# Thirty-two early rows of a weight matrix: from partitions four apart in two regions to partitions eight apart in one

## The chip, the cores and the metric

One core of a Trainium2 chip runs the kernel. The metric is device microseconds of one execution, as a median over executions; lower is better. TensorE (PE) multiplies matrices into PSUM, VectorE (DVE) and ScalarE (ACT) compute, GpSimd (POOL) fills constants, and SyncE (SP) issues nearly all transfers from device memory (HBM) to on-chip memory (SBUF, 128 partitions). The core has 16 DMA engines.

## The reference

One decode step for 8 sequences, in float32. The layer-normed input feeds attention over a given cache and a dense layer with the Mish activation; both are added to the input.

```python
x = A_x                                   # (8, 1, 512)
xn = layernorm(x)
q = (xn @ wq)                             # 32 heads of 128
k, v = k_cache, v_cache                   # (8, 8 kv heads, 8192, 128), 4 query heads on each
p = softmax(q @ k^T * 128**-0.5)
a = (p @ v) @ wo                          # wo: (4096, 512)
h = xn @ w1 + b1                          # 512 -> 1792
b = (h * tanh(softplus(h))) @ w2          # 1792 -> 512
return x + a + b
```

The two caches are 2 x 268 MB; everything else that is read is about 24 MB.

## The kernel before

The work is cut into 32 units `j` (4 pairs of key/value heads by 8 sequences, `b = j % 8`). Each unit has a load of keys and a load of values, 8.4 MB each, as tiles of 128 partitions by 16384 floats (`load_unit`); they share the tile `kv`, in which each load waits until the tensor before it has been consumed. In one turn of the loop PE does the scores of unit `j` (L339), the softmax's small steps, the values of unit `j - 1` (L411), and a turning of the weights `e` (L378); SP issues the value load of `j`, then extra transfers if there are any, and in the next turn the key load of `j + 2`. SP issues its transfers in program order, and one that waits for a buffer holds those behind it.

After the loop come `wo` in four tiles (L634), `w2` in five pieces (L640), and the output. The sum of the four `wo` products, two per head pair and row block, is built up in the PSUM tile `H` (`few`, `outputs`, `down_long`), then folded to `O`, to which the last pieces of `w2` are added (L567) before VectorE adds the input (L664) and SP stores it.

**The early rows.** Each tile of `wo` is 128 partitions of four pieces of 1024 floats. Of head pair 0 the fourth piece of all rows, and of pair 1 the last 384 floats of it (`FEWC`), are not loaded after the loop with the rest but during it: `FEW1` and `FEW2` list small transfers, `load_few` issues them behind the value load of the unit given in the list. They go into `ws`, the tile of `wq`, which is free by then. There are 32 rows `q` of each pair, and a row of the transfer is four runs of 4 KB (pair 0) or of 1.5 KB (pair 1). A transfer has `k` = 5 or 3 rows; in the program's reckoning its first row is one share of work, its second row another, and so on.

Before, a transfer's rows stand four partitions apart, from partition `t` (0 to 3) for the five-row ones. The three-row ones stand from partition 32 + `t` for pair 0; for pair 1 they stand at `t` too, in a second slot further along the partition. `turn_few(m)` brings the attention output of the pair into the matching order with two matmuls against columns of the identity (20 and 12 rows), each followed by a VectorE copy to `oF`. `few(m)` multiplies: eight products over 44 rows for pair 0, at the end of unit 27; eight over 20 rows for pair 1, after the loop.

Counting a row of pair 0 as 1 and one of pair 1 as 384/1024 = 0.375, the five places of a transfer carry 11, 11, 11, 5.5 and 5.5 of 44.

Of the kernel before, what the change touches and what calls it, by code (L numbers as in the profile page):

```python
# [8 lines left out]
F32 = mybir.dt.float32  # L9
# [4 lines left out]
P = 128  # L14
B = 8
D = 512
# [8 lines left out]
G = 4  # L25
NH = 2
TG = SK // (NH * G) // P
BW = 1024
CC = D // P
FG = F // G  # L30
FT = 4
FP = FG // FT
Q = P // G
# [33 lines left out]

FEW1 = [(t, 5, t, 22 + t // 2, 0) for t in range(4)]  # L70
FEW1 += [(32 + t, 3, 20 + t, 24 + t // 2, 0) for t in range(4)]
FEW2 = [(t, 5, t, 28 + t // 2, 0) for t in range(4)]
FEW2 += [(t, 3, 20 + t, 30, 1) for t in range(4)]
EARLY = 27
FEWC = 384

# [5 lines left out]
def kernel(  # L82
# [12 lines left out]
    nc = tc.nc  # L95
    PSUM = bass.MemoryType.PSUM

    const = ctx.enter_context(tc.tile_pool(name="const", bufs=1))
# [5 lines left out]
    ws = const.tile([P, CC * BW], F32, name="ws")  # L104
# [4 lines left out]
    M = psum.tile([P, 512], F32, name="m")  # L109
    H = psum.tile([P, 512], F32, name="h")  # L110

    ident = const.tile([P, P], F32, name="ident")
# [12 lines left out]
    oT = const.tile([P, H2, B], F32, name="oT")  # L125
# [1 line left out]

    x8 = oX.rearrange("p m i h b -> p (m i h b)")[:, : W1R * 2 * B]
    x8 = x8.rearrange("p (i h b) -> p i h b", i=W1R, h=2)
    oF = const.tile([48, 2, CC, 2, B], F32, name="oF")  # L130
    aT = const.tile([P, 2 * W2R, B], F32, name="aT")
    pt8 = const.tile([P, HALF, PL * TL, H2], F32, name="pt8")
    tr = const.tile([P, PL * TL, 32], F32, name="tr")
# [1 line left out]
    def load_q(m):  # L135

        rows = wq.rearrange("j p f -> (j p f)").rearrange("(m p f) -> m p f", m=NP, p=P)
        nc.sync.dma_start(ws, rows[m])

    def load_unit(src, j, at):  # L140
        m, b = divmod(j, B)
        lo = (b * HKV + 2 * m) * NH * G
        t = kv[:, at : at + ROW]
        nc.sync.dma_start(
            t,
            src[lo : lo + NB].rearrange("j p f -> (j p f)").rearrange("(p f) -> p f", p=P),
        )
        return t
# [7 lines left out]
    rows = wq.rearrange("j p f -> (j p f)").rearrange("(m p f) -> m p f", m=NP, p=P)[0]  # L156
# [2 lines left out]
    nc.scalar.dma_start(ws[:, half:], rows[:, half:])  # L159
    b1_sb = kv[:G, W1_AT + 7168 : W1_AT + 7168 + FG]  # L160

    for lo in range(0, FG, 150):
        hi = min(lo + 150, FG)
        nc.scalar.dma_start(b1_sb[:, lo:hi], b1.rearrange("(g f) -> g f", g=G)[:, lo:hi])
    k_t = {0: load_unit(kT, 0, V_AT)}
    w1_t = kv[:, W1_AT : W1_AT + 7168].rearrange("p (i f) -> p i f", i=W1R)
# [3 lines left out]
    nc.gpsimd.memset(ones, 1.0)  # L170
    nc.gpsimd.memset(perm, 0.0)
    nc.gpsimd.memset(pt8, 0.0)
    nc.gpsimd.memset(oF, 0.0)
    for t in (H, M):
        nc.vector.memset(t, 0.0)
    nc.vector.reduce_sum(bsel, ident.rearrange("p (g q) -> p q g", g=G), axis=AX.X)
# [1 line left out]
    def more_constants():  # L178
        nc.vector.reduce_sum(mask, ident.rearrange("p (x d) -> p x d", x=NB), axis=AX.X)
        nc.vector.reduce_sum(  # L180
            hmask, ident.rearrange("p (c h q) -> p h c q", c=CC, h=2), axis=AX.XY
        )
        nc.vector.memset(O, 0.0)
        for g in range(4):

            src = ident.rearrange("p (c d u g h) -> p d u g c h", c=2, d=2, u=2, g=4)
            dst = perm[:, g].rearrange("p (d u g c h) -> p d u g c h", d=2, u=2, g=4, c=2)
            for d in range(2):
                nc.vector.tensor_copy(dst[:, d, :, g], src[:, d, :, g])
        nc.vector.reduce_sum(hsel, ident.rearrange("p (c h) -> p h c", h=H2), axis=AX.X)  # L190
        nc.vector.reduce_sum(
            isel, ident.rearrange("p (c t h) -> p t c h", t=TL, h=H2), axis=AX.XY
        )
        for d in range(2):
            nc.vector.reduce_sum(
                rsel[:, d * REP : (d + 1) * REP],
                ident.rearrange("p (c d k h) -> p d h c k", c=2, d=2, h=REP)[:, d],
                axis=AX.XY,
            )
        nc.vector.tensor_copy(  # L200
            gsel, ident[:G, :G].rearrange("p (g o) -> p g o", o=1).to_broadcast([G, G, B])
        )
# [128 lines left out]
    def scores(j, k, first, part):  # L331

        w = WK[j]
        lo = 0 if first else DI // 2
        kk = k.rearrange("p (i c f) -> p i c f", i=DI, c=HALF)
        for n in range(DI // 2):
            i = lo + n
            for c in range(HALF):
                nc.tensor.matmul(  # L339
                    S[64 * c : 64 * (c + 1), :],  # L340
                    w[:, i].rearrange("p d k h -> p (d k h)"),
                    kk[:, i, c, :],
                    start=(part == 0 and n == 0),
                    stop=(part == 1 and n == DI // 2 - 1),
                )
# [80 lines left out]
    def merge(j, os):  # L426
        m, b = divmod(j, B)
        nc.tensor.matmul(M[:, 168 : 168 + H2], os, hsel, start=True, stop=True)  # L428
        nc.vector.tensor_mul(oT[:, :, b], M[:, 168 : 168 + H2], RT.pop(j))
# [61 lines left out]
        nc.vector.tensor_copy(aT, turned.rearrange("p (j q) -> p j q", q=Q)[:, :, :B])  # L491


    def load_few(m, p, k, q, slot):

        rows = wo[4 * m : 4 * (m + 1)].rearrange("u p f -> (u p f)")
        rows = rows.rearrange("(u q i f) -> q u i f", u=4, i=4, f=BW)
        n = FEWC if m else BW
        t = ws[p : p + 4 * k - 3 : 4, 4 * n * slot : 4 * n * (slot + 1)].rearrange(
            "p (u f) -> p u f", u=4  # L500
        )
        nu = 2 if m and k == 5 else 4
        for u in range(0, 4, nu):
            nc.sync.dma_start(
                t[:, u : u + nu], rows[q : q + 4 * k - 3 : 4, u : u + nu, 3, BW - n :]
            )

    def turn_few(m):

        o = oT.rearrange("p h b -> p (h b)")  # L510
        n = H2 * B
        parts = ((0, 20, 0, 0), (0, 12, 20, 1) if m else (32, 12, 20, 0))
        for p, r, lo, slot in parts:
            t = M[p : p + r, 384 + n * slot : 384 + n * (slot + 1)]
            nc.tensor.matmul(t, ident[:, 4 * lo + 3 : 4 * (lo + r) : 4], o, start=True, stop=True)
            if m:
                nc.vector.tensor_copy(
                    oF[p : p + r, 1].rearrange("p u h b -> p (u h b)").rearrange(
                        "p (s u b) -> p s u b", s=2, u=CC
                    )[:, slot],  # L520
                    t.rearrange("p (u h b) -> p u h b", u=CC, h=2)[:, :, 1],
                )
            else:
                nc.vector.tensor_copy(oF[p : p + r, 0].rearrange("p u h b -> p (u h b)"), t)

    def few(m):
        rows = (44, 20)[m]
        n = FEWC if m else D
        w = oF[:rows, m].rearrange("p u h b -> p (u h b)").rearrange("p (n b) -> p n b", b=B)
        for i in range(2 * CC):  # L530
            nc.tensor.matmul(
                H[Q * (i % G) : Q * (i % G) + B, D - n :],
                w[:, i],
                ws[:rows, i * n : (i + 1) * n],
                start=(m == 0 and i < G),
                stop=False,
            )

# [45 lines left out]
    for j in range(UNITS):  # L584
        b = j % B
        more = j // B + 1 < NP

        k = k_t.pop(j)
        low_first = j == 0 or j % 2 == 1
        scores(j, k, low_first, 0)  # L590
        if j == UNITS - 1:
            v_t[j] = load_unit(v, j, K_AT[0])
        elif j > 0:
            k_t[j + 1] = load_unit(kT, j + 1, K_AT[(j + 1) % 2])
        scores(j, k, not low_first, 1)
        WK.pop(j)
        softmax(j)
        os = None
        if j > 0:
            os = values(j - 1, v_t.pop(j - 1))  # L600
        if j > B and b == 1:
            turn_o(j // B - 1)
        if j == B + 1 or j == 2 * B + 1:
            turn_few(j // B - 1)
        if j + 1 < UNITS:
            v_t[j] = load_unit(v, j, V_AT)
            if more and b == SPREAD_Q:
                spread(qT)
            key_weights(j + 1)
        if j == 0:  # L610
            mish(w1_t, b1_sb, kv[:, W1_AT : W1_AT + 6 * FG])
        for m, rows in enumerate((FEW1, FEW2)):
            for p, k, q, at, slot in rows:
                if j == at:
                    load_few(m, p, k, q, slot)
        if more and b == LOAD_Q:
            load_q(j // B + 1)
        if more and b == MAKE_Q:
            qT = project(tr.rearrange("p y c -> p (y c)")[:, :512])
        turn(j)  # L620
        if j > 0:
            merge(j - 1, os)
        if more and b == SPREAD_Q - 1:
            selections()
        if j == EARLY:
            few(0)
# [3 lines left out]
    for m in range(NP):  # L630
        rows = wo[4 * m : 4 * (m + 1)].rearrange("u p f -> (u p f)")
        rows = rows.rearrange("(p f) -> p f", p=P)
        n = (3 * BW, 4 * BW - FEWC)[m] if m < 2 else 4 * BW
# [3 lines left out]
    parts = ((0, G), (G, 8), (8, 11), (11, 13), (13, 14))  # L637
    for lo, hi in parts:
        t = kv[:, W2_AT + lo * D : W2_AT + hi * D]
# [13 lines left out]
    for g in range(G):  # L653
# [4 lines left out]
            start=True,  # L658
            stop=False,
# [44 lines left out]
```

## Time and profile before

| | us |
|---|---|
| median of 3 runs | 1309.56 (1309.19 to 1310.08) |
| profiled execution, its own time | 1309.29 |
| its span, first to last instruction | 1307.5 |
| PE busy | 1087.8 (83%) |
| DVE busy | 346.4 (26%) |
| ACT busy | 44.4 (3%) |
| DMA, mean over the span | 430 GB/s |

Busy times are sums over an engine's instructions; a share of DMA is the mean over the 16 DMA engines. A view by windows gives, for a stretch of time, each compute engine's busy time with its instruction count, the clock granted to TensorE, the DMA engines' mean busy share and their rate. The chain of waits is followed back from the last instruction: each piece is either work or the transfer that was waited for.

### The profile page before, as it was taken

Reading aid. Unit: us, or ns where it says so; the run is one execution under the profiler, and the core shown is the slowest. Engines: PE = TensorE matmul, PEld = TensorE weight load, DVE = VectorE, ACT = ScalarE, POOL = GpSimd, SP = SyncE. Lnnn points to the kernel's source line nnn. Section 1 sums busy time; section 2 is a strip of 40 time slices with the busy share of each in tenths; the row PEclk is TensorE's granted clock in tenths of the full one; section 3 lists DMA queues with packets and bytes.
Section 4 is the critical chain, followed back from the end, with each engine's and each line's share of the span. In section 5 each row is a group of like instructions: output and inputs, shape, how many; then the busy total and the mean of one; then the engine's idle time right before and its main releaser. Section 6 shows DMA issues by size and latency. Waiting matters only on the chain.

```text
span 1307.5 us, 11114 instructions
## 1 busy us (share of the span) xinstructions
PE 1087.8 (83%) x5088; PEld 352.2 (27%) x5088; DVE 346.4 (26%) x547; ACT 44.4 (3%) x121; POOL 2.3 (0%) x10
## 2 busy tenths in 40 slices
PE   6988888878979789787887888787897797888786
PEld 4222222223323222222322222232232222222222
DVE  3341222321223221223131222212322311323212
ACT  1000000000000000000000000000000000000000
POOL 0000000000000000000000000000000000000000
PEclk9999888898989898888898888897988997988898
DMA  9999999999999999999999999999999999999998
GB/s 404 444 422 442 428 437 429 435 435 430 430 437 430 436 431 436 428 438 432 432 434 430 438 426 444 422 442 426 437 428 434 435 427 440 428 434 427 435 433 339
DMA packets 11946, 561.79 MB, mean 430 GB/s; under 512 B 1384, under 2 KB 1652, under 8 KB 2172
## 3 DMA queue, kind: packets, MB, share of 16 engines
q1 hardware_dynamic: 11732, 560.03, 99.2%
q10 hardware_dynamic: 168, 1.06, 0.2%
q8 instruction: 40, 0.66, 0.2%
q14 instruction: 6, 0.05, 0.0%
HBM read 561.01 MB, written 0.07 MB: 429 GB/s over the span
## 4 chain that ended last, share of the span: by engine, by line
DMA 72%; PE 26%; DVE 1%; issue 0%; ACT 0%; SPq 0%
DMA kv<-in_v 64%; PE o L411 18%; DMA kv<-in_kT 6%; PE s L339 6%; DMA kv<-in_w 2%; PE x L378 2%; PE h L457 1%; PE x L303 0%; DVE tr L394 0%; DVE nm L351 0%; DVE tr L396 0%; ACT qr L310 0%; PE o L567 0%; PE h L452 0%; DVE nr L355 0%
## 5 line engine op out<-in xcount | busy, mean ns | idle before, releaser
L339 PE MATMUL s<-kv,wk 128*64 128x512 f32 x2048 | 501.4, 652 | 90.0 <-DMA kv<-in_kT 51.0
L411 PE MATMUL o<-kv,pt 128*32 128x512 f32 x2048 | 267.0, 681 | 48.5 <-DMA kv<-in_v 45.7
L339 PEld LDWEIGHTS s<-kv,wk 128*64 128x64 f32 x2048 | 164.3, 151 | 404.4 <-issue 317.8
L378 PE MATMUL x<-e,perm 128*128 128x512 f32 x256 | 228.0, 1046 | 2.0 <-ACT qr L310 2.0
L351 DVE TENSOR_REDUCE nm<-s 128x1 f32<-128x512 f32 x32 | 22.1, 692 | 432.5 <-PE s L339 432.5
L411 PEld LDWEIGHTS o<-kv,pt 128*32 128x32 f32 x2048 | 69.7, 123 | 220.2 <-issue 168.2
L378 PEld LDWEIGHTS x<-e,perm 128*128 128x128 f32 x256 | 53.3, 219 | 143.1 <-issue 140.5
L394 DVE STREAM_TRANSPOSE tr<-x 128x2048 f32<-128x2048 f32 x32 | 73.1, 2285 | 54.4 <-PE x L378 54.4
L419 DVE TENSOR_SCALAR os<-o,isel 128x128 f32<-128x128 f32 x32 | 11.2, 351 | 275.3 <-PE o L411 275.3
L322 DVE TENSOR_TENSOR wk<-qr,mask 128x1024 f32<-128x1024 f32 (+1 forms) x33 | 62.8, 1902 | 18.7 <-ACT qr L310 18.7
L400 DVE TENSOR_TENSOR pt<-tr 64x512 f32<-64x512 f32 x64 | 43.9, 686 | 1.6
L367 ACT COPY nmx<-m 128x1 f32<-128x1 f32 x32 | 5.1, 159 | 1111.3 <-PE m L363 1111.3
L396 DVE TENSOR_TENSOR tr<-tr 128x1024 f32<-128x1024 f32 x32 | 39.2, 1225 | 1.1
L421 DVE SCALAR_TENSOR_TENSOR os<-o,isel,os 128x128 f32<-128x128 f32 x96 | 33.7, 351 | 3.4
L352 PE MATMUL m<-ident,nm 128*1 128x128 f32 x32 | 8.6, 270 | 25.3 <-DVE nm L351 25.3
L392 DVE RECIPROCAL rt<-m 128x16 f32<-128x16 f32 x16 | 4.1, 258 | 78.6 <-PE m L388 78.6
L363 PE MATMUL m<-ident,nx 1*128 1x1 f32 x32 | 7.0, 217 | 19.8 <-DVE nx L357 19.8
L370 ACT ACTIVATE e<-s,nmx 128x512 f32<-128x512 f32 x32 | 22.0, 687 | 1.0
L303 PE MATMUL x<-qT,tr 128*128 128x64 f32 x128 | 19.3, 315 | 3.0 <-ACT qr L310 2.7
L303 PEld LDWEIGHTS x<-qT,tr 128*128 128x128 f32 x128 | 18.1, 226 | 6.2 <-ACT qr L310 3.3
L428 PEld LDWEIGHTS m<-hsel,os 128*128 128x128 f32 x64 | 11.2, 196 | 27.6 <-issue 19.5
L373 DVE TENSOR_SCALAR lsel<-rsel,l 128x8 f32<-128x8 f32 x32 | 7.4, 231 | 42.0 <-ACT e L370 42.0
(107 smaller groups left out, 180.8 us busy)
## 6 DMA issues: line engine op xcount, KB each, us to landing
ws<-in_wq SPq DMA_DIRECT2D x3, 2048.0 KB
kv<-in_wo SPq DMA_DIRECT2D x2, 2048.0 KB
kv<-in_w SPq DMA_DIRECT2D x1, 3584.0 KB
kv<-in_w SPq DMA_DIRECT2D x2, 1024.0 KB
kv<-in_wo SPq DMA_DIRECT2D x1, 1856.0 KB
kv<-in_wo SPq DMA_DIRECT2D x1, 1536.0 KB
ws<-in_wq ACTq DMA_DIRECT2D x1, 1024.0 KB
ws<-in_wq SPq DMA_DIRECT2D x1, 1024.0 KB
```

Of the source, the lines that this page charges most:

```text
L303: nc.tensor.matmul(X[:, half, k * 64 : (k + 1) * 64], wide[:, half * 8 + k], qT, start=True, stop=True,)
L322: nc.vector.tensor_mul(w[:, i : i + n], q[:, i : i + n].to_broadcast([P, n, 2, NH * G, REP]), mask.rearrange("p (o d k r) -> p o d k r", o ...
L339: nc.tensor.matmul(S[64 * c : 64 * (c + 1), :], w[:, i].rearrange("p d k h -> p (d k h)"), kk[:, i, c, :], start=(part == 0 and n == 0), s ...
L351: nc.vector.tensor_reduce(nm, S, axis=AX.X, op=ALU.max, negate=True)
L370: nc.scalar.activation(e, S, AF.Exp, bias=nmx, accum_out=l)
L378: nc.tensor.matmul(X[:, g], perm[:, g], e.rearrange("p (t q l) -> p l t q", t=TL, q=PP), start=True, stop=True,)
L394: nc.vector.transpose(tr, X.rearrange("p g (y q) -> p y g q", q=PP))
L396: nc.vector.tensor_add(t[:, :, 0], t[:, :, 0], t[:, :, 1])
L400: nc.vector.tensor_add(pt8[half, :, :, d * REP : (d + 1) * REP].rearrange("p c y h -> p y c h"), t[:, 0], t[:, 1],)
L411: nc.tensor.matmul(O[Q * q : Q * (q + 1), :], pt8[:, c, TL * l : TL * (l + 1), :].rearrange("p t h -> p (t h)"), vt[:, 512 * n : 512 * (n ...
L421: nc.vector.scalar_tensor_tensor(os, O[:, DH * i : DH * (i + 1)], isel[:, i : i + 1], os, op0=ALU.mult, op1=ALU.add)
L457: nc.tensor.matmul(hp[Q * g : Q * g + B, :], x8[:, i, g // 2], w1_t[:, i, g % 2 * FG : (g % 2 + 1) * FG], start=False, stop=(i == W1R - 1),)
```

## The change

The rows stay the same 32 of each pair and so do their bytes; the places change. One list `FEW` holds for each pair its groups (first partition, width, rows per transfer, first row), and `FEW_AT` the unit behind which each transfer is issued. A transfer's rows now stand eight partitions apart. For pair 0 the five-row transfers start at partitions 0 to 3 and the three-row ones at 4 to 7, so that they interleave in one region of 36 partitions. For pair 1 there are six five-row transfers, starting at 0 to 5, and one of two rows, at 6 and 14, in a region of 38. The five places of a transfer now carry 10.625, 10.625, 10.25, 6.25 and 6.25.

`turn_few` uses one matmul against a selection matrix `fsel`, made at the start by four VectorE copies from the identity into a tile that GpSimd zeroes (it used to zero `oF`), and one copy. `few(1)` has four products over 38 rows in place of eight over 20. The small vector `b1` comes in two transfers on ACT's queue in place of three.

```diff
-FEW1 = [(t, 5, t, 22 + t // 2, 0) for t in range(4)]
-FEW1 += [(32 + t, 3, 20 + t, 24 + t // 2, 0) for t in range(4)]
-FEW2 = [(t, 5, t, 28 + t // 2, 0) for t in range(4)]
-FEW2 += [(t, 3, 20 + t, 30, 1) for t in range(4)]
+FEW = (((0, 4, 5, 0), (4, 4, 3, 20)), ((0, 6, 5, 0), (6, 1, 2, 30)))
+FEW_AT = ((22, 22, 23, 23, 24, 24, 25, 25), (28, 28, 29, 29, 30, 30, 30))
+FEWP = (36, 38)
...
-    for lo in range(0, FG, 150):
-        hi = min(lo + 150, FG)
+    for lo in range(0, FG, FG // 2):
+        hi = lo + FG // 2
...
-    nc.gpsimd.memset(oF, 0.0)
+    nc.gpsimd.memset(fsel, 0.0)
...
+        rows = ident.rearrange("p (q i) -> p i q", i=4)[:, 3]
+        for m in range(2):
+            for p, w, k, q in FEW[m]:
+                nc.vector.tensor_copy(
+                    fsel[:, m].rearrange("p (n t) -> p n t", t=8)[:, :k, p : p + w],
+                    rows[:, q : q + w * k].rearrange("p (n t) -> p n t", t=w),
+                )
...
-    def load_few(m, p, k, q, slot):
+    def load_few(m, p, k, q, w):
...
-        t = ws[p : p + 4 * k - 3 : 4, 4 * n * slot : 4 * n * (slot + 1)].rearrange(
-            "p (u f) -> p u f", u=4
-        )
+        t = ws[p : p + 8 * k - 7 : 8, : 4 * n].rearrange("p (u f) -> p u f", u=4)
+        last = q + w * (k - 1) + 1
...
-                t[:, u : u + nu], rows[q : q + 4 * k - 3 : 4, u : u + nu, 3, BW - n :]
+            nc.sync.dma_start(t[:, u : u + nu], rows[q:last:w, u : u + nu, 3, BW - n :])
...
     def turn_few(m):
-        parts = ((0, 20, 0, 0), (0, 12, 20, 1) if m else (32, 12, 20, 0))
-        for p, r, lo, slot in parts:
...
+        r = FEWP[m]
+        t = M[:r, 384 : 384 + n]
+        nc.tensor.matmul(
+            t, fsel[:, m, :r], oT.rearrange("p h b -> p (h b)"), start=True, stop=True
+        )
+        nc.vector.tensor_copy(oF[:r, m].rearrange("p u h b -> p (u h b)"), t)
...
     def few(m):
-        for i in range(2 * CC):
+        for i in range(m, 2 * CC, 1 + m):
+            q = i // (1 + m)
             nc.tensor.matmul(
-                H[Q * (i % G) : Q * (i % G) + B, D - n :],
-                w[:, i],
-                ws[:rows, i * n : (i + 1) * n],
+                H[Q * (q % G) : Q * (q % G) + B, D - n :],
+                oF[: FEWP[m], m, i // 2, i % 2],
+                ws[: FEWP[m], q * n : (q + 1) * n],
```

On SP, from the value load of unit 29 to the first tile of `wo`, the program before reads as follows (a row is a line, the tile written and the tensor read, the shape, and a count):

```order
L144 DMA kv<-in_v 128x16384
L504 DMA ws<-in_wo 5x2x384 x4
L144 DMA kv<-in_kT 128x16384
L144 DMA kv<-in_v 128x16384
L504 DMA ws<-in_wo 3x4x384 x4
L144 DMA kv<-in_v 128x16384
L634 DMA kv<-in_wo 128x3072
```

And now:

```order
L146 DMA kv<-in_v 128x16384
L513 DMA ws<-in_wo 5x2x384 x4
L146 DMA kv<-in_kT 128x16384
L146 DMA kv<-in_v 128x16384
L513 DMA ws<-in_wo 5x2x384 x4
L513 DMA ws<-in_wo 2x4x384
L146 DMA kv<-in_v 128x16384
L633 DMA kv<-in_wo 128x3072
```

Behind the value load of unit 30 stand five small transfers in place of four; all others keep their place and shape, and only the partitions they write differ, which such rows do not show.

On PE, from the last turning of the weights to the fold into `O`, before (`pt`: the turned weights, `os` and `oT`: the attention output):

```order
L378 MATMUL x_69<-e,perm 128x512 x4
L388 MATMUL m<-lsel,ones 128x16
L428 MATMUL m<-hsel,os 128x8
L531 MATMUL h<-ws,oF 8x384 x8
L411 MATMUL o<-kv,pt_90 32x512 x32
L544 MATMUL h<-kv,oX 8x512 x6
```

And now:

```order
L388 MATMUL x_69<-e,perm 128x512 x4
L398 MATMUL m<-lsel,ones 128x16
L438 MATMUL m<-hsel,os 128x8
L529 MATMUL h<-ws,oF 8x384 x4
L421 MATMUL o<-kv,pt_91 32x512 x32
L542 MATMUL h<-kv,oX 8x512 x6
```

Four products fewer stand ahead of the last unit's values; nothing else there has moved.

More of the change, by code (lines that the diff above doesn't have):

```diff
@@ L129 @@
     x8 = x8.rearrange("p (i h b) -> p i h b", i=W1R, h=2)
-    oF = const.tile([48, 2, CC, 2, B], F32, name="oF")
+    oF = const.tile([FEWP[1], 2, CC, 2, B], F32, name="oF")
+    fsel = const.tile([P, 2, 40], F32, name="fsel")
     aT = const.tile([P, 2 * W2R, B], F32, name="aT")
@@ L498, in load_few @@
         n = FEWC if m else BW
-        t = ws[p : p + 4 * k - 3 : 4, 4 * n * slot : 4 * n * (slot + 1)].rearrange(
-            "p (u f) -> p u f", u=4
-        )
+        t = ws[p : p + 8 * k - 7 : 8, : 4 * n].rearrange("p (u f) -> p u f", u=4)
+        last = q + w * (k - 1) + 1
         nu = 2 if m and k == 5 else 4
         for u in range(0, 4, nu):
-            nc.sync.dma_start(
-                t[:, u : u + nu], rows[q : q + 4 * k - 3 : 4, u : u + nu, 3, BW - n :]
-            )
+            nc.sync.dma_start(t[:, u : u + nu], rows[q:last:w, u : u + nu, 3, BW - n :])
     def turn_few(m):
-        o = oT.rearrange("p h b -> p (h b)")
         n = H2 * B
-        parts = ((0, 20, 0, 0), (0, 12, 20, 1) if m else (32, 12, 20, 0))
-        for p, r, lo, slot in parts:
[L514 to L524, printed above, removed]
+        r = FEWP[m]
[4 more added lines that the diff above has]
+        nc.vector.tensor_copy(oF[:r, m].rearrange("p u h b -> p (u h b)"), t)
     def few(m):
-        rows = (44, 20)[m]
         n = FEWC if m else D
-        w = oF[:rows, m].rearrange("p u h b -> p (u h b)").rearrange("p (n b) -> p n b", b=B)
-        for i in range(2 * CC):
+        for i in range(m, 2 * CC, 1 + m):
+            q = i // (1 + m)
             nc.tensor.matmul(
-                H[Q * (i % G) : Q * (i % G) + B, D - n :],
-                w[:, i],
-                ws[:rows, i * n : (i + 1) * n],
-                start=(m == 0 and i < G),
+                H[Q * (q % G) : Q * (q % G) + B, D - n :],
+                oF[: FEWP[m], m, i // 2, i % 2],
+                ws[: FEWP[m], q * n : (q + 1) * n],
+                start=(m == 0 and q < G),
                 stop=False,
@@ L611 @@
             mish(w1_t, b1_sb, kv[:, W1_AT : W1_AT + 6 * FG])
-        for m, rows in enumerate((FEW1, FEW2)):
-            for p, k, q, at, slot in rows:
+        for m in range(2):
+            rows = [(p + t, k, q + t, w) for p, w, k, q in FEW[m] for t in range(w)]
+            for row, at in zip(rows, FEW_AT[m]):
                 if j == at:
-                    load_few(m, p, k, q, slot)
+                    load_few(m, *row)
         if more and b == LOAD_Q:
```

## The prediction

> **What bounds the kernel now.** I read the page first, then the chain of waits, then the DMA engines' share by windows. The page:
>
> ```profile
> span 1307.5 us, 11114 instructions
> PE 1087.8 (83%) x5088; PEld 352.2 (27%) x5088; DVE 346.4 (26%) x547; ACT 44.4 (3%) x121; POOL 2.3 (0%) x10
> DMA packets 11946, 561.79 MB, mean 430 GB/s; under 512 B 1384, under 2 KB 1652, under 8 KB 2172
> q1 hardware_dynamic: 11732, 560.03, 99.2%
> q8 instruction: 40, 0.66, 0.2%
> DMA 72%; PE 26%; DVE 1%; issue 0%; ACT 0%; SPq 0%
> ```
>
> Queue q1, the one on which SP issues, fills 99.2% of the 16 DMA engines' time; 72% of the chain is transfers. PE is busy for 83%, but waits for loads in every unit. Only the DMA engines have no time left, so the end is set by whichever of the sixteen has most to do. The last pieces of the chain:
>
> ```profile
> 918.23 28.57 DMA kv<-in_v
> ...
> 1247.45 30.05 DMA kv<-in_v
> 1277.51 25.93 DMA kv<-in_w
> 1303.49 0.62 PE o L567 x16
> 1304.12 0.45 PE o L567 x8
> 1304.60 0.29 DVE os L664
> ```
>
> The last piece of `w2` lands at 1303.45 us and 1.4 us of work and the store follow. How the sixteen end is seen in windows (us of each engine, granted clock, DMA share, GB/s), with one window of the steady part ahead:
>
> ```profile
> 600.00:640.00 40.00, 34.37 (x153) 10.49 (x145) 11.92 (x16) 0.94 (x3) 0.00 (x0) 0.87 0.98 425
> 1297.20:1298.90 1.70, 1.21 (x12) 0.12 (x8) 0.00 (x0) 0.00 (x0) 0.00 (x0) 1.00 0.88 366
> 1300.40:1301.80 1.40, 1.06 (x32) 0.77 (x32) 0.00 (x0) 0.00 (x0) 0.00 (x0) 1.00 0.75 307
> 1302.00:1302.90 0.90, 0.66 (x24) 0.55 (x24) 0.00 (x0) 0.00 (x0) 0.00 (x0) 1.00 0.67 271
> 1303.00:1303.20 0.20, 0.09 (x4) 0.00 (x0) 0.00 (x0) 0.00 (x0) 0.00 (x0) 1.00 0.56 215
> 1303.20:1303.40 0.20, 0.00 (x0) 0.00 (x0) 0.00 (x0) 0.00 (x0) 0.00 (x0) 1.00 0.41 154
> 1303.40:1303.60 0.20, 0.11 (x4) 0.11 (x8) 0.00 (x0) 0.00 (x0) 0.00 (x0) 1.00 0.11 41
> 1303.60:1304.30 0.70, 0.69 (x24) 0.34 (x17) 0.00 (x0) 0.00 (x0) 0.00 (x0) 1.00 0.00 0
> ```
>
> In the steady part a busy engine moves 425 / (0.98 x 16) = 27.1 GB/s. At the end the share says how many still work: 14 of 16 after 1297.2, 12 after 1300.4, 11 after 1302.0, 9 after 1303.0, none after 1303.6. So two engines are 6 us ahead of the last, and about eleven end within 1.6 us of each other. The early rows use this lead: they put work on a few engines so that all have less at the end. In no row has an engine a name; I take it, as the program reckons, that row `i` of a small transfer is carried by engine `i`, so that 5 engines carry extra rows and 11 carry none.
>
> **The change, part by part.**
>
> *The shares.* A row of pair 0 is 4 x 4096 B, at 27.1 GB/s 0.60 us of an engine; one of pair 1, 4 x 1536 B, is 0.23 us. Engines 0 and 1 carry 0.375 x 0.60 = 0.23 us less, engine 2 carries 0.45 us less, engines 3 and 4 carry 0.45 us more; 11 engines carry the same. Of the nine that still work at 1303.0 at most three can be ones that lose work, so the others still end near 1303.5. I count 0; the bounds are a gain of 0.2 us (were the last ones engines 0 to 2) and a loss of 0.3 us (were engine 3 or 4 among them).
>
> *The partitions.* This is the part that can cost. A full load gives each engine eight of the 128 partitions. I take as working picture that these are four neighbours and the four that lie 32 higher, and call such a set an entry: engine `e` fills entry `e`, which for the first 32 partitions is p // 4. No row shows it. Then before, every early row lay in the entry of the engine that carried it (t + 4i and 32 + t + 4i). Now pair 0's five-row transfers lie in entries 0, 2, 4, 6, 0 and its three-row ones in 1, 3, 5; of pair 1 those from partitions 0 to 3 lie as the former, those from 4 and 5 in 1, 3, 5, 7, 1, and the last two rows in 1 and 3. In rows of pair 0, engine 1 carries 10.6 rows, all into entries that other engines fill, and its own entry takes 5.9 rows from others; for engine 2 it is 10.25 out and 5.5 in; for engine 4, 6.25 and 5.5; for 3, 6.25 and 5.1; for 0, 5.1 and 5.5.
>
> What sharing an entry costs, no row of this trace can show, since before nothing shares. If 27.1 GB/s is all that an entry takes in, then a row that meets the main stream takes twice its 0.60 us, and the entry's own engine loses 0.60 us as well. Ceiling, if every row meets a stream: engine 1 loses (10.6 + 5.9) x 0.60 = 10.0 us, engine 2 loses 9.5 us. Floor: a row meets none while the entry's engine is itself away with early rows. That can't be for engine 2's second-group rows (entry 5, whose engine carries no early rows: 4 + 2 x 0.375 = 4.75 rows) nor for engine 1's in entry 3 in the three-row and two-row transfers (4.4 rows), so at least 4.75 x 0.60 = 2.9 us. I take the middle, 6.4 us: the rows of one unit keep an engine about 1.2 us, and the windows show engines up to 6 us apart, so bursts that could miss each other will often not coincide. If instead 27.1 GB/s is the engine's own limit and the entry takes more, the cost is 0.
>
> The row says 27.1 GB/s for each busy engine and not where the limit sits. [...]
>
> *SP.* The early transfers keep their place behind the value loads; at unit 30 five stand in place of four.
>
> ```profile
> 1226.41 0.33 SPq L144 DMA_DIRECT2D kv<-in_v  x1
> 1226.79 3.05 SPq L504 DMA_DIRECT2D ws<-in_wo  x4
> 1247.45 0.34 SPq L144 DMA_DIRECT2D kv<-in_v  x1
> ```
>
> Four issues take 3.05 us here, so a fifth 0.8 us, and SP then stands until 1247.45: at least 16 us of cover (1229.84 to 1247.45), 0 on the path. Were the cover gone, the last value load would be issued 0.8 us later. The region for pair 1 lies where pair 0's was, as before, and waits for the same products of unit 27.
>
> *PE and VectorE.* `few(1)` loses half its products:
>
> ```profile
> 1274.78 1.66 PE L531 MATMUL h<-ws,oF 20*8 20x384 f32 x16
> 1279.31 8.77 PE L411 MATMUL o<-kv,pt 128*32 128x512 f32 x64 [2.88 <-DVE pt L400]
> ```
>
> It saves 0.8 us, and PE then waits 2.88 us for VectorE's L400 anyway: it will wait 3.7 us, and the path has nothing of it. The turning saves one matmul and one copy for each pair:
>
> ```profile
> L515 PE MATMUL m<-oT,ident 128*20 128x64 f32 x4 | 0.7, 270 | 4.0 <-DVE oX L444 4.0
> L515 PE MATMUL m<-oT,ident 128*12 128x64 f32 x4 | 0.7, 264 | 0.6 <-DVE oF L524 0.4 <-DVE oF L517 0.3
> ```
>
> That is 0.7 us of PE and 0.6 us of waiting over both pairs, behind the values and ahead of the next load's landing: 0, bounded by 1.3 us of gain if it stood on the path. Four new VectorE copies stand in the start, ahead of the query's copy:
>
> ```profile
> 2.74 0.20 POOL L173 MEMSET oF<- 48x128 f32 x1
> 12.07 0.62 DVE L189 COPY perm<-ident 128x16 f32<-128x16 f32 x8
> 17.55 0.22 DVE L296 TENSOR_SCALAR qT<-m 128x64 f32<-128x64 f32 x1 [3.95 <-PE m L288]
> 27.94 2.83 PE L339 MATMUL s<-kv,wk 128*64 128x512 f32 x6 [0.60 <-DMA kv<-in_kT]
> ```
>
> Eight like them took 0.62 us in a row, one by itself about 0.15, so four take 0.3 to 0.6 us. They need GpSimd's zeroes, which by the row of `oF` are there by 3 us, and lie ahead of 3.95 us in which VectorE waits for PE; the first scores wait for a load in the end. Cost 0; without that cover 0.6 us. One ACT-queue transfer less for `b1`: 0.
>
> *Sum.* The delayed engine starts from 0 to 0.5 us ahead of the last (the three windows from 1303.0), and gets up to 0.2 us from the new shares: I take 0.5 off. 1309.29 + 6.4 - 0.5 = 1315.2 us against the profiled execution's own time, which is 1.8 us over its span and 0.27 us under the median of the runs; on the median's scale **1315.5 us**. The bounds of this case are 2.9 - 0.5 and 10.0 - 0.5, so 1312.0 to 1319.1.
>
> **The rivals.**
>
> *An entry takes more than one engine gives.* Then the partitions don't matter and only the shares move: 1309.4 us, from 1309.3 to 1309.9. For it: every engine runs at the same 27.1 GB/s whatever it loads, as it would with a limit of its own. Against it: the same holds with a limit at the entry. It decides if an entry takes 54 GB/s or more; I give it 0.22.
>
> *An entry has a part to spare.* With room for one and a half streams a shared row takes a third longer, and the entry's engine loses as little: about a third of 10.0 us at most and of 2.9 us at least, 1.0 to 3.3 us, in the middle 2.2 less 0.5: 1311.3 us. I give it 0.12.
>
> *The delay feeds on itself.* A late engine delays every landing, so PE, so the next issue. From unit 22 on the shortest wait of the chain for a value load is 28.57 us, of which 8.4 MB at 16 x 27.1 GB/s take 19.3 us: 9.2 us were still queued when it was issued, and only a delay beyond this lets the late engine itself run dry. At the ceiling of 9.5 us that is 0.3 us in each of ten units, 3 us more: 1322. I give it 0.02.
>
> *A gain over 0.2%* (2.6 us, about what a measurement of this kernel can tell from no change) would need the eleven unchanged engines to have less to do. Their bytes are the same; 0.2 us of shares and 1.3 us of PE, all put on the path, don't reach it: 0.02.
>
> **How the numbers follow.** The forecast's case has 0.62. Faster by over 0.2%: 0.02. Within 0.2% of 1309.56, so up to 1312.2: all of the first rival and 0.05 of the second, 0.27. Slower: the forecast's 0.62, 0.07 of the second and 0.02 of the third, 0.71. The range must reach the first rival, since without it 0.22 and more would be left out: from 1309.0. At the top I cut the last microsecond of the ceiling: 1318.2. By itself the likeliest case has 1312.0 to 1319.1.
>
> **What would show it.** Right: from unit 22 on, a stretch with early rows moves fewer bytes for the same DMA share; at the end the share falls to 0.06 to 0.3 (one to five engines) near 1303.6 and stays there until 1306 to 1313, while the chain's last `w2` piece lands that much later. Wrong: the windows at the end read as before, 9 engines after 1303.0 and none after 1303.6 us. The step that then failed is the sharing, not the shares. PE's wait before the last values should read 3.7 us, VectorE's before L306 about 3.4 us; if the first scores start later than 27.94 us, the start was not covered.

## The result and the profile after

The changed kernel takes 1316.47 us (median of 6 runs, 1315.91 to 1317.48) where the kernel before took 1309.58 us on the same chip (6 runs, 1309.19 to 1310.34): ratio 1.0053, 95% interval 1.004 to 1.0066, so 6.9 us slower. The profiled execution took 1315.91 us, 6.6 us over that of before. The page of the changed kernel:

```profile
span 1314.1 us, 11089 instructions
PE 1094.5 (83%) x5076; PEld 353.1 (27%) x5076; DVE 346.2 (26%) x549; ACT 44.6 (3%) x121; POOL 2.3 (0%) x10
DMA packets 11947, 561.77 MB, mean 427 GB/s; under 512 B 1390, under 2 KB 1654, under 8 KB 2174
q1 hardware_dynamic: 11742, 560.03, 99.1%
```

Queue q1 moves the same 560.03 MB at the same share (99.2% before) in a span that is 6.6 us longer. The engines are not idle for longer, they are slower. The end of the chain of waits says the same:

```profile
1253.47 30.84 DMA kv<-in_v
1284.34 25.96 DMA kv<-in_w
1310.34 0.62 PE o L565 x16
1310.97 0.45 PE o L565 x8
1311.44 0.29 DVE os L663
```

The last piece of `w2` lands at 1310.30 us, 6.85 us later than before. What is behind it is as it was. Where the time goes is seen in windows (us and instructions of PE, PE's weight load, DVE, ACT and POOL; granted clock; DMA share; GB/s), first the units with the early rows, before:

```profile
930.00:1280.00 350.00, 293.53 (x1342) 92.94 (x1342) 89.89 (x137) 9.60 (x29) 0.00 (x0) 0.89 1.00 431
```

and after, with the end:

```profile
930.00:1280.00 350.00, 297.69 (x1318) 91.62 (x1315) 84.38 (x130) 9.64 (x29) 0.00 (x0) 0.88 1.00 425
1303.00:1303.60 0.60, 0.60 (x10) 0.12 (x4) 0.00 (x0) 0.00 (x0) 0.00 (x0) 1.00 0.88 369
1307.00:1308.00 1.00, 0.78 (x31) 0.77 (x32) 0.00 (x0) 0.00 (x0) 0.00 (x0) 1.00 0.73 297
1308.00:1309.00 1.00, 0.28 (x12) 0.00 (x0) 0.00 (x0) 0.00 (x0) 0.00 (x0) 1.00 0.45 180
1309.00:1310.00 1.00, 0.84 (x24) 0.55 (x24) 0.00 (x0) 0.00 (x0) 0.00 (x0) 1.00 0.24 94
1310.00:1310.50 0.50, 0.16 (x8) 0.17 (x12) 0.00 (x0) 0.00 (x0) 0.00 (x0) 1.00 0.13 49
```

From unit 22 on, the DMA engines move 425 GB/s where they moved 431, at a share of 1.00 in both. At the end, before, 9 engines worked just after 1303.0 and none after 1303.6; now 14 work there, 12 from 1307 to 1308, 7 in the next microsecond, 4 in the next. Not a few engines are late, but nearly all.

### The profile page after: what moved, and what is told of

Same layout as the page of the kernel before. It is cut to its first block, busy times and chain, and to the rows that moved or that the text cites. A ratio compares the mean times of both kernels' runs of the same rounds, so it can differ in the third digit from the quotient of the medians.

```text
span 1314.1 us, 11089 instructions
## 1 busy us (share of the span) xinstructions
PE 1094.5 (83%) x5076; PEld 353.1 (27%) x5076; DVE 346.2 (26%) x549; ACT 44.6 (3%) x121; POOL 2.3 (0%) x10
## 3 DMA queue, kind: packets, MB, share of 16 engines
q1 hardware_dynamic: 11742, 560.03, 99.1%
## 4 chain that ended last, share of the span: by engine, by line
DMA 75%; PE 24%; DVE 0%; issue 0%; SPq 0%
DMA kv<-in_v 66%; PE o L421 18%; DMA kv<-in_kT 7%; PE s L349 4%; DMA kv<-in_w 2%; PE x L388 1%; PE h L467 1%; DVE tr L404 0%; DVE nm L361 0%; DVE tr L406 0%; PE h L462 0%; PE o L565 0%; DVE nr L365 0%; PE m L362 0%; DVE nx L367 0%
## 5 line engine op out<-in xcount | busy, mean ns | idle before, releaser
L421 PE MATMUL o<-kv,pt 128*32 128x512 f32 x2048 | 272.0, 692 | 53.1 <-DMA kv<-in_v 49.3
```

The costliest lines, as they stand in the source:

```text
L421: nc.tensor.matmul(O[Q * q : Q * (q + 1), :], pt8[:, c, TL * l : TL * (l + 1), :].rearrange("p t h -> p (t h)"), vt[:, 512 * n : 512 * (n ...
```

## The experiments

All are compared with the kernel before, run on the same chip beside them. "Foreign" is a row that its engine writes into an entry of another engine, in the prediction's picture of entries: four neighbouring partitions and the four 32 higher. "Own" is a row in the entry of the engine that carries it. No view names an engine: both words rest on the prediction's numbering, and the runs bear it out by times alone. With the rows four apart from partitions 0 and 32, own by it, the time was that of before (1309.46 us); with the three-row ones of pair 0 moved from 32 to 52 it was 2.4 us longer, with all rows moved by four partitions 10.1 us. All but two keep the change's selection matrix and its single product per turning; a fifth number in the groups is the distance between a transfer's rows.

**The new shares with every row in its own entry.** Pair 1 has the change's six five-row transfers and one of two rows, but rows are four partitions apart again:

```diff
-FEW = (((0, 4, 5, 0), (4, 4, 3, 20)), ((0, 6, 5, 0), (6, 1, 2, 30)))
+FEW = (((0, 4, 5, 0, 4), (32, 4, 3, 20, 4)), ((0, 4, 5, 0, 4), (32, 2, 5, 20, 4), (34, 1, 2, 30, 4)))
```

> The changed kernel with its new shares, its selection matrix and its single matmul and copy for each pair, but with the rows put back four partitions apart, so that each engine writes its own entry (five-row transfers from 0 to 3, three-row ones from 32 on; of pair 1 the last two five-row transfers and the two-row one from 32 on). Theory (sharing of entries costs all of it): as the kernel before, 1309.4 us, from 1309.1 to 1309.9. Rival (the new shares, the order of the transfers or the selection matrix cost it): 1316.5 us.

Measured: 1309.46 us (11 runs, 1309.18 to 1310.67), ratio 1.0 (0.9991 to 1.0009). Its chain and an end window:

```profile
1277.60 25.97 DMA kv<-in_w
```

```profile
1303.00:1303.60 0.60, 0.19 (x8) 0.00 (x0) 0.00 (x0) 0.00 (x0) 0.00 (x0) 1.00 0.45 171
```

The last load lands as before, at 1303.57, and no engine works much longer than before. The shares, the selection matrix, the four copies at the start and the fifth transfer at unit 30 are worth nothing that can be measured; the partitions are worth all of it.

**The old shares, eight partitions apart.**

```diff
-FEW = (((0, 4, 5, 0), (4, 4, 3, 20)), ((0, 6, 5, 0), (6, 1, 2, 30)))
+FEW = (((0, 4, 5, 0, 8), (4, 4, 3, 20, 8)), ((0, 4, 5, 0, 8), (4, 4, 3, 20, 8)))
```

> The changed kernel with the old list of transfers for pair 1 (four of five rows, four of three), so with the old shares 11, 11, 11, 5.5 and 5.5, at eight partitions apart. Theory (sharing): 1316.5 us, within 1 us of the changed kernel, since the rows outside their own entry are as many. Rival (the new shares cost it): 1309.6 us.

Measured: 1317.17 us (4 runs, 1316.62 to 1317.21), ratio 1.0056 (1.0042 to 1.007). The partitions alone cost 7.6 us.

**Twelve foreign rows, into entries whose engines carry no early rows.** Only the four three-row transfers of pair 0 move, to partitions 52 to 55 and four and eight higher, entries 5 to 7:

```diff
-FEW = (((0, 4, 5, 0), (4, 4, 3, 20)), ((0, 6, 5, 0), (6, 1, 2, 30)))
+FEW = (((0, 4, 5, 0, 4), (52, 4, 3, 20, 4)), ((0, 4, 5, 0, 4), (32, 4, 3, 20, 4)))
```

> Old list and four partitions apart, all in their own entries but for the four three-row transfers of pair 0, which start at partitions 52 to 55 and so lie in entries 5, 6 and 7, whose engines carry no early rows and are ahead. It prices one shared row: engines 0 to 2 have 4 such rows each, always against a full stream. Theory (an entry takes 27.1 GB/s and is shared evenly): each loses 4 x 0.60 = 2.4 us, of which up to 0.5 us is lead: 1311.5 to 1312.0 us. An entry with room for one and a half streams: a third, 0.8 us, so 1309.9 to 1310.4. No sharing: 1309.4.

Measured: 1312.04 us (10 runs, 1311.71 to 1313.11), ratio 1.0019 (1.001 to 1.0028). The time came out as expected of a full price. The windows at its end did not look as pairs of engines would make them:

```profile
1303.00:1303.60 0.60, 0.57 (x24) 0.57 (x28) 0.00 (x0) 0.00 (x0) 0.00 (x0) 1.00 0.79 328
1305.00:1305.50 0.50, 0.50 (x24) 0.43 (x16) 0.00 (x0) 0.00 (x0) 0.00 (x0) 1.00 0.73 287
1306.00:1306.50 0.50, 0.35 (x15) 0.34 (x16) 0.00 (x0) 0.00 (x0) 0.00 (x0) 1.00 0.03 12
```

Twelve engines are at work until 1305.5 and none after 1306.1. Were only engines 0 to 2 and 5 to 7 late, at most six could be at work there. It is the end of before, about 2.5 us later.

**Every row foreign, one entry up.** The old shares, four partitions apart, all moved up by four partitions, so that engine `i` writes into entry `i` + 1 (the lists of the kernel before, partly shown, and this kernel's):

```diff
-FEW1 = [(t, 5, t, 22 + t // 2, 0) for t in range(4)]
-FEW1 += [(32 + t, 3, 20 + t, 24 + t // 2, 0) for t in range(4)]
...
+FEW = (((4, 4, 5, 0, 4), (36, 4, 3, 20, 4)), ((4, 4, 5, 0, 4), (36, 4, 3, 20, 4)))
```

> Old list and old shares, four partitions apart, but all moved up by four partitions, so that engine i writes entry i + 1. It tells how often bursts meet: engine 2's 5.5 three-row rows go to entry 3, whose engine has none then, and are shared for certain, 3.3 us; the ceiling is engines 1 and 2 with 11 rows out and 11 in, 13.3 us. Theory: between 1312.4 and 1322.6; near the lower end if the engines' bursts coincide in time, in the middle (1317.5) if they mostly miss each other as I took for the forecast. No sharing: 1309.4.

Measured: 1319.73 us (4 runs, 1319.36 to 1322.9), ratio 1.0084 (1.0069 to 1.01); above the middle of what was expected, inside its ends. Its end has two parts:

```profile
1306.50:1307.00 0.50, 0.50 (x9) 0.12 (x4) 0.00 (x0) 0.00 (x0) 0.00 (x0) 1.00 0.77 311
1307.50:1308.00 0.50, 0.29 (x4) 0.00 (x0) 0.00 (x0) 0.00 (x0) 0.00 (x0) 1.00 0.37 152
1309.00:1310.00 1.00, 0.30 (x4) 0.00 (x0) 0.00 (x0) 0.58 (x1) 0.00 (x0) 1.00 0.20 82
1312.00:1313.00 1.00, 0.49 (x20) 0.49 (x24) 0.00 (x0) 0.00 (x0) 0.00 (x0) 1.00 0.11 45
```

Most engines end some 4 us later than before, and then three, later two, go on until 1313.7.

**Eight rows a transfer, all own.** Built on the kernel before: transfers of eight rows, so on engines 0 to 7, each in its own entry; pair 1's fourth piece goes early whole, and one `few()` with 64 rows stands after the loop. If engines 5 to 7 have a lead, as the theory takes 0 to 4 to have, this takes bytes off every engine that ends last.

```diff
-    def load_few(m, p, k, q, slot):
+    def load_few(m, t):
...
+        p = Q * m + t
+        dst = ws[p : p + 29 : 4].rearrange("p (u f) -> p u f", u=4)
+        nc.sync.dma_start(dst, rows[t : t + 29 : 4, :, 3])
```

> From the kernel before: early rows in transfers of eight rows, four partitions apart from partition t (pair 0) and 32 + t (pair 1), so engines 0 to 7 carry one row each of every transfer and write only their own entries; pair 1's fourth piece is now early as a whole (1024 floats in place of 384), one transfer behind each value load of units 22 to 29, and eight products over 64 rows stand ahead of the last values in place of few(0) and few(1). Theory (in the windows before, five engines with early rows and three without end at or ahead of eight others, so without early rows all of 0 to 7 would be some 6 us ahead): 8 rows x 0.60 = 4.8 us fit into the lead, and every engine has 32 x 10240 B / 16 = 20 KB less after the loop, 0.76 us: 1308.8 us, from 1308.5 to 1309.1. Rival (the engines that are ahead without early rows are not 5 to 7): an engine without a lead gets 4.8 us more, less 0.76: 1313.5 us.

Measured: 1314.2 us (5 runs, 1313.81 to 1314.85), ratio 1.0034 (1.0021 to 1.0047). The theory fell and its rival stands. The window shows who is late:

```profile
1306.00:1307.00 1.00, 0.31 (x12) 0.32 (x16) 0.00 (x0) 0.00 (x0) 0.00 (x0) 1.00 0.12 49
```

0.12 of 16 is two engines, working alone until about 1307.9. Eight rows of 0.60 us are 4.8 us on an engine that ends at 1303.5 anyway, less 0.75 us that the larger early part takes off every engine (32 rows with 0.625 of a row more, 12 us over sixteen): 1307.55 by this estimate. So, by the numbering, two of engines 5 to 7 have no lead.

**The same with the bytes of before.** As the last one with 384 floats of pair 1, so 5.5 rows on each of engines 0 to 7.

```diff
-        dst = ws[p : p + 29 : 4].rearrange("p (u f) -> p u f", u=4)
-        nc.sync.dma_start(dst, rows[t : t + 29 : 4, :, 3])
+        dst = ws[p : p + 29 : 4, : 4 * n].rearrange("p (u f) -> p u f", u=4)
+        nc.sync.dma_start(dst, rows[t : t + 29 : 4, :, 3, BW - n :])
```

> As eight_rows, but of pair 1 only the last 384 floats are early, as in the kernel before, so the bytes after the loop are those of before and only the shares differ: engines 0 to 7 carry 5.5 rows each in place of 11, 11, 11, 5.5 and 5.5 on five. Theory (eight engines without early rows end last, whatever the others' shares are up to 11): 1309.4 us, from 1309.1 to 1309.7, and at the end half of the engines stop about 3 us ahead of the other half. Rival (engines 0 to 2 with 11 rows set the end): 1308.9 us or less.

Measured: 1313.25 us (8 runs, 1312.91 to 1313.5), ratio 1.0027 (1.0016 to 1.0037). It missed for the same reason: 5.5 x 0.60 = 3.3 us on engines without a lead, 1309.5 + 3.3 = 1312.8. Its end, too, shows about two engines alone:

```profile
1305.00:1306.00 1.00, 0.20 (x12) 0.07 (x8) 0.00 (x0) 0.00 (x0) 0.00 (x0) 1.00 0.11 45
```

Engines 0 to 4 carry no more here than before, so the late ones are among 5 to 7. Both are losses by shares alone, with every row own, and their ends show two engines late; the change's end shows nearly all.

**Eight foreign rows: one entry or eight.** By now the question was how the cost of a foreign row is spread. Eight rows of pair 0 go on engines 0 and 1, four each in four two-row transfers, either all into entry 9 or one each into entries 8 to 15; no engine of these carries early rows. Everything else is own. The groups of pair 0, first in the kernel with own entries and new shares, then in these two kernels (the groups of pair 1 are left out):

```diff
-FEW = (((0, 4, 5, 0, 4), (32, 4, 3, 20, 4)), ...
+FEW = (((0, 4, 5, 0, 4), (68, 1, 2, 20, 1), (70, 1, 2, 22, 1), (100, 1, 2, 24, 1), (102, 1, 2, 26, 1), (32, 1, 4, 28, 4)), ...
+FEW = (((0, 4, 5, 0, 4), (64, 1, 2, 20, 4), (72, 1, 2, 22, 4), (80, 1, 2, 24, 4), (88, 1, 2, 26, 4), (32, 1, 4, 28, 4)), ...
```

> From the layout with every row in its own engine's entry and the new shares of pair 1. Of pair 0, eight rows (20 to 27) go as four two-row transfers, so on engines 0 and 1 and four rows each, two transfers behind unit 24 and two behind unit 25, all into one entry: number 9 (partitions 68 to 71 and 100 to 103), whose engine carries no early rows. The last four rows go as one four-row transfer in own entries behind unit 23. Engines 0 and 1 then carry 11.6 rows where they carried 10.6 to 11, which is 0.1 to 0.4 us by itself: 1309.6 to 1309.9 us if sharing cost nothing. Theory A (in a burst all sixteen engines lose the extra time of the most loaded foreign entry): a burst has four rows of 0.60 us in one entry, 2.4 us, and there are two bursts: 4.8 us, so 1314.4 us; the whole end is later, with a share of 0.4 or more at 1306, and from 1016 to 1028 us fewer than 4.8 MB for the same share. Theory B (only the entry's own engine and the ones that intrude lose): engine 9 loses 4.8 us, engines 0 and 1 as much between them at least, 2.4 to 4.8 each: 1312 to 1314.4 us, but with at most three engines (share 0.19) at work after 1304, and from 1016 to 1028 us 5.0 MB or more.

> As the kernel with all eight rows in entry 9, same transfers on the same engines 0 and 1, but the eight rows go one each to the eight entries 8 to 15 (partitions 64, 68 to 92), whose engines carry no early rows. Theory A (all lose the extra time of the most loaded foreign entry): a burst has one row of 0.60 us in any entry, so two bursts cost 1.2 us: 1310.7 to 1311.1 us, over 3 us under the kernel with one entry. Theory B (only the entry's own engine and the ones that intrude lose): engines 0 and 1 lose 4 x 0.60 = 2.4 us each, the others 0.6: about 1312.0 us, with two engines (share 0.13) alone at the end. If sharing costs nothing: 1309.6 to 1309.9 us.

Measured: one entry 1314.36 us (4 runs, 1314.33 to 1315.59), ratio 1.004 (1.0025 to 1.0055); eight entries 1311.58 us (10 runs, 1311.08 to 1312.82), ratio 1.0017 (1.0008 to 1.0027). The ends, of one entry:

```profile
1303.50:1304.00 0.50, 0.49 (x8) 0.00 (x0) 0.00 (x0) 0.00 (x0) 0.00 (x0) 1.00 0.66 266
1306.00:1307.00 1.00, 0.44 (x17) 0.15 (x8) 0.00 (x0) 0.00 (x0) 0.00 (x0) 1.00 0.19 76
1308.00:1308.50 0.50, 0.08 (x4) 0.00 (x0) 0.00 (x0) 0.00 (x0) 0.00 (x0) 1.00 0.10 37
```

and of eight entries:

```profile
1303.50:1304.00 0.50, 0.50 (x29) 0.50 (x20) 0.00 (x0) 0.00 (x0) 0.00 (x0) 1.00 0.62 254
1304.50:1305.00 0.50, 0.00 (x0) 0.00 (x0) 0.00 (x0) 0.00 (x0) 0.00 (x0) 1.00 0.56 217
1305.50:1306.00 0.50, 0.41 (x16) 0.12 (x6) 0.00 (x0) 0.00 (x0) 0.00 (x0) 1.00 0.14 53
```

Both theories fall in part. With one entry the time is that of theory A, 1314.4 us, but its end is not: the mass of engines ends at about 1304.7, less than 2 us late, and three, later two, go on alone to 1308.4, as theory B had it. With eight entries nine engines work until 1305, some 2 us late, where theory A had 1.2 us; the two stragglers of theory B are there (a share of 0.14), but alone for less than 1 us, until 1306.2. From 1016 to 1028 us the two kernels moved 4.92 and 4.98 MB, under the 5.0 of theory B and over the 4.8 of theory A. So a foreign row had two costs here: one borne by nearly all engines, and one more borne by the engines that meet in an entry, which shows where it goes to the same few.

**What one foreign row costs.** The transfers of one unit with early rows, from 1016 to 1028 us, by the DMA view (queue q1: packets, MB, share of 16 engines in the 12 us). The kernel with the new shares and own entries has six own rows there (the kernel before reads 5.14 MB at 99.2%):

```profile
q1 hardware_dynamic: 124, 5.21, 100.5%
```

The kernel with three-row transfers into entries 5 to 7 has six foreign ones:

```profile
q1 hardware_dynamic: 117, 4.75, 102.1%
```

Engines that are busier move 9% less. The same view over the whole stretch from 930 to 1300 us reads, with the new shares and own entries:

```profile
q1 hardware_dynamic: 3888, 158.97, 99.6%
```

with eight entries:

```profile
q1 hardware_dynamic: 3799, 158.42, 99.7%
```

with one entry:

```profile
q1 hardware_dynamic: 3755, 158.29, 99.8%
```

with three-row transfers into entries 5 to 7:

```profile
q1 hardware_dynamic: 3747, 158.12, 99.8%
```

in the changed kernel:

```profile
q1 hardware_dynamic: 3554, 156.89, 99.9%
```

with the old shares eight apart:

```profile
q1 hardware_dynamic: 3508, 156.59, 99.8%
```

and with all moved by one entry:

```profile
q1 hardware_dynamic: 3517, 156.64, 99.8%
```

With own entries, 99.6% of 16 x 370 us for 158.97 MB is 37.1 us of an engine for each MB. What another kernel's busy time has above 37.1 us for each of its MB is lost to sharing (each share is rounded to 0.1%, 6 us of engine time, so the differences are good to about 6 us). Rows of pair 1 count as 0.375:

| kernel | foreign rows | engine time lost, us | for each row | a sixteenth of it | slower than before, us |
|---|---|---|---|---|---|
| eight entries | 8 | 25 | 3.1 | 1.6 | 2.2 |
| one entry | 8 | 36 | 4.5 | 2.2 | 4.9 |
| three-row ones into 5 to 7 | 12 | 42 | 3.5 | 2.6 | 2.4 |
| the change | 38.5 | 93 | 2.4 | 5.8 | 6.9 |
| old shares, eight apart | 38.5 | 99 | 2.6 | 6.2 | 7.6 |
| all moved by one entry | 44 | 97 | 2.2 | 6.1 | 10.1 |

A foreign row of 0.60 us costs the sixteen engines together 2.2 to 4.5 us. If only its engine and the entry's own engine lost 0.60 us each, it would be 1.2. A sixteenth of the loss is what the end would move if all bore it alike; that gives the time within 0.2 to 1.4 us, but for one entry and for all moved by one entry, which are the two whose last windows show few engines alone.

The traces also hold each packet's own start, duration and size, which the views add up. A packet of 64 KB, one partition's part of a load of keys or values, takes 2.42 us there, and one of 4 KB, a quarter of an early row of pair 0, 0.16 us. With own entries no 64 KB packet that starts from 1016 to 1028 us takes over 2.43 us. In the kernel with one entry fourteen are in flight at 1022 us, as many as there are engines without early rows at that time: one takes 4.97 us and the others 2.59 to 2.96. In the kernel with three-row transfers into entries 5 to 7 thirteen are in flight then, and all take 3.01 to 3.84 us, though only three engines can own these entries. Of the 48 foreign packets of 4 KB there 25 take 0.32 to 0.34 us, twice their usual time; where two engines write into the one entry beside its owner they take up to 0.54 us. So those that meet in an entry pay about what the prediction worked out for them (4.97 - 2.42 = 2.55 us for four rows of 0.60), and the others pay too. Summed from 930 us on, what the packets take beyond their usual time, less the same sum with own entries, is 27, 35, 37, 91, 99 and 97 us in the order of the table, within 5 us of its column of time lost.

That engines other than the two that meet are slowed is shown. How one engine's row holds up another that writes elsewhere is not: with three-row transfers into entries 5 to 7 each row cost 3.5 us of engine time and twelve engines were late, but no run here separates one cause of it from another. Nor do the runs tell how the loss depends on how many engines carry foreign rows at a time.

No run points to a version that beats both kernels: the one with own entries and new shares is equal to the kernel before, within 0.1%.

## Why the prediction was right, and where not

- **The time and its cause.** 1315.5 us were forecast and 1316.47 measured, in the likeliest case's own range. Rows in entries of other engines are the cause: undone, they leave 1309.46.
- **The shares** were counted at 0, between -0.2 and +0.3 us. With own entries they are worth 1309.46 against 1309.61 us, nothing that can be measured.
- **The price of the partitions** was taken at 6.4 us less 0.5 of lead, 5.9; it measured 6.9 (6.6 between the profiled executions). The step that failed is how it arises: that a shared row costs its own engine and the entry's engine 0.60 us each and the others nothing, so that 2.9 to 10.0 us fall on a few engines. The price for these two is borne out by the packets, the nothing for the others is not. By that step it would be 38.5 x 1.2 = 46 us of engine time in all; 93 were lost, spread over nearly all engines, 5.8 us each, and the unevenness adds the rest. That the middle of the bracket came so near is in part luck: fewer engine microseconds than were lost, laid on fewer engines than bore them.
- **What would show it.** Fewer bytes for the same share from unit 22 on: 425 against 431 GB/s, as forecast. A share of 0.06 to 0.3 near 1303.6: wrong, it was 0.88, since 14 engines were late. The last piece between 1306 and 1313: it landed at 1310.30.
- **The rivals.** An entry that takes 54 GB/s would have left 1309.4: it doesn't. A part to spare, 1311.3: no, a foreign packet that meets one stream takes 0.32 to 0.34 us in place of 0.16, not a third longer. That the delay feeds on itself needed an engine more than 9.2 us late; the last one was 6.85 us late.
- **The entries.** The runs agree that four neighbouring partitions are one place where engines meet: the same rows moved by four partitions cost 10.1 us, and in own entries nothing; eight rows put into one such place cost 4.9 us, spread over eight 2.2. That an entry takes in 27.1 GB/s and no more, on which the 6.4 us rest, was the author's assumption, and no run shows it by itself. For the engines that meet, packets of 0.32 to 0.34 us in place of 0.16 agree with it; that the others lose too, with packets of 3.01 to 3.84 us in place of 2.42, does not follow from it.

**The covers** held. SP's five issues took 3.77 us where 3.85 were worked out, and it stood again until 1253.47, 16 us:

```profile
1233.21 0.33 SPq L146 DMA_DIRECT2D kv<-in_v  x1
1233.59 3.77 SPq L513 DMA_DIRECT2D ws<-in_wo  x5
1253.47 0.34 SPq L146 DMA_DIRECT2D kv<-in_v  x1
```

On PE `few(1)` takes 0.83 us less, and the wait ahead of the last values reads 3.70 us, as forecast:

```profile
1281.09 0.83 PE L529 MATMUL h<-ws,oF 38*8 38x384 f32 x8
1285.62 8.77 PE L421 MATMUL o<-kv,pt 128*32 128x512 f32 x64 [3.70 <-DVE pt L410]
```

The start was covered too: the first scores begin at 27.77 us (27.94 before). VectorE's four copies took 0.44 us, within 0.3 to 0.6. Its wait read 4.32 us, not 3.4: the copies ahead of it came 0.9 us earlier than before (`perm` at 11.18, not 12.07), which I had not counted.

```profile
11.18 0.62 DVE L191 COPY perm<-ident 128x16 f32<-128x16 f32 x8
11.73 0.44 DVE L196 COPY fsel<-ident 128x20 f32<-128x20 f32 x4
...
17.39 0.22 DVE L306 TENSOR_SCALAR qT<-m 128x64 f32<-128x64 f32 x1 [4.32 <-PE m L298]
...
27.77 1.97 PE L349 MATMUL s<-kv,wk 128*64 128x512 f32 x4 [0.58 <-DMA kv<-in_kT]
```

## What to carry to other kernels

When all DMA engines are full, place each row of a small side transfer in the partitions that its own engine fills in the large loads; where the rows land can cost more than their bytes. Here, with q1 at 99.2%, 38.5 foreign rows made the kernel 7.6 us slower (old shares, eight apart): 2.6 us of engine time lost for each, beside its own 0.60. Read the end by the share of engines still at work: a share of 0.1 to 0.2 that lasts is a few late engines (0.12 with eight own rows a transfer, a matter of shares; 0.19 with one entry, where foreign rows met). A whole end moved later at the same shape, as by 2.5 us with three-row transfers into entries 5 to 7, was here a rate that nearly all had lost, and a stretch with more busy time for each MB said where (4.75 MB at 102.1% against 5.21 at 100.5%). Before relying on the leads of particular engines, measure each one's with a run that loads it.

## What was not expected of the hardware

- A row of 4 x 4096 B into an entry that another engine is filling cost the sixteen engines 2.2 to 4.5 us together, 3.7 to 7.5 times its own 0.60 us, and slowed engines that neither carry it nor own the entry: with foreign rows of three engines in the entries of three others, all thirteen 64 KB packets in flight at 1022 us took 3.01 to 3.84 us in place of 2.42.
- Of engines 5 to 7, by the prediction's numbering, two have no lead at the end: 5.5 more rows on each of engines 0 to 7, every one in its own entry, cost 3.7 us. Which engines have the lead of 6 us, and what gives it to them, was not tried.
